# Induced-set attention with a folded feed-forward layer: the second attention in token order, scores lowered in PSUM, most natural x transposed on chip

## The chip, the cores and the metric

One core of a Trainium2 chip runs the whole program. The metric is device time in microseconds of that core; the kernel before takes 263.87 us (median of 3 runs, 262.73 to 266.32). Smaller is better. The engines are named PE (matrix products; PEld its loads of the stationary operand), DVE, ACT, POOL and SP, which issues all transfers here.

## The reference

```
B, N, m, C = 4, 12480, 32, 128        # x [B,N,C] f32, inducing [m,C]; w_in [128,2048], w_out [2048,128]
def mab(q, kv):
    s = (q @ kv.T) / sqrt(C)
    a = exp(s - s.max(-1));  a /= a.sum(-1) + 1e-9
    return a @ kv
h = mab(inducing, x)                  # per batch: 32 rows attend to 12480 tokens
y = mab(x, h)                         # 12480 tokens attend to 32 rows
u = y @ w_in
out = (u - tanh(u)) @ w_out           # [49920, 128] f32
```

The inputs x and inducing are drawn with a spread of 0.1, the weights are handed to the program in their drawn width of 64 bits, as pairs of 32-bit words. Since the rows of h lie close together, both kernels put the layer u - tanh(u) as a tangent around the mean of the 32 rows: 32 rows P of 128 values then stand for h after the layer, and the second attention yields the output as a weighted mean of the rows of P. A bound on the error is worked out in the program (`bound`), and where it does not hold, a general branch (`general`, under `tc.If`) computes everything in full. It is not taken with these inputs.

## The kernel before

The input comes in two layouts: `xT` with the 128 channels on the partitions, and `xn`/`xl`, natural x with tokens on the partitions. Each batch of 12480 tokens is cut into six segments of 1920 tokens (four quarters of SEG = 480) and one of 960 (two quarters).

`first(b)` is the first attention. For each segment `xT` is loaded (L279), `scores` (L260, L263) makes four products of 480 columns, each on its own 32 columns of the array, so that four quarters stand on 128 partitions of one PSUM bank, and DVE copies them with a running maximum (L290). When all seven are there, the maximum goes through a transpose and four tiny products to `nb` (L299 to L309). Then natural x is loaded (L315), ACT takes the exponentials (L322), DVE transposes blocks of 32x32 (L326), and 15 products of 32 stationary columns gather `hacc` (L333). From it come h, transposed (`hT4s[b]`, L342 to L353).

`linear(b)` (L362) multiplies h with the weights: 16 products with 128 stationary columns of `win_sb` and 32 moving columns (L367), mean, tanh and a series on DVE and ACT, the tangent `W` (L404, L405), 16 products with `wout_sb` (L416), and the fold to `P4` (L419, L421).

`second(b, s)` is the second attention, in `b_chain` (L449): scores with `hT4s` (L263), a DVE transpose to tokens on the partitions (L455), maximum (L457), subtraction on POOL (L462), exponentials on ACT (L464), sum (L467), reciprocal (L472, L473), scaling on POOL (L475), a transpose back (L478), and the products with the stationary `P4`, four of 480 columns and 32 rows, two and two into a tile `o` (L496; two such tiles). ACT evicts each half (L502) into `ot`, and SP stores it channel by channel (L505, `outT`).

`weight` (L207) loads the weights as words in eight blocks (L218) and makes 32-bit floats of them: two ACT operations (L221, L236), five on DVE (L224 to L232), two on POOL (L239, L242).

The order on every engine is fixed when the program is built: `Plan.order` takes each operation with a cost, an engine, buffers and a priority (smaller goes first), plays the engines through in time, and writes the instructions down in the order of the starts it found. An engine that waits for an operation's input holds everything behind it. Buffers come from places counted in `PLACES`: 11 for `xT`, 5 for `xn`, 3 for `ot`, 4 PSUM banks (`ps`), 2 tiles `o` of two banks. `first(b)` has priorities from 100b, `second(b, s)` from 100(b + 1) + 13s, so the second attention of one batch is mixed with the first of the next. The loads of w_in start at -30.5, those of w_out at -26.5, those of batch 0's `xT` at -30.

## Time and profile before

| | |
|---|---|
| runs, median (lowest to highest) | 263.87 us (262.73 to 266.32) |
| profiled execution, span | 267.4 us |
| PE, DVE, ACT, POOL busy | 75%, 64%, 37%, 29% |
| mean granted clock of PE | 0.830 |
| read and written in HBM | 55.33 MB, 25.56 MB |

The span goes from the first to the last instruction of one execution on the chip. It is the profiled execution's own time; what lies around the span is not given apart, and the span is 1.3% above the median of the runs. L12 is line 12 of the kernel. A group's row has, after the line: engine, operation, output<-input, shapes, count, then busy time in us and the mean of one in ns, then the idle time before them and what ended it. In a row of the order of time, the first number is the start, the second the length, both in us. A product in full precision appears as two pairs of a load and a multiplication, so that 4 products are x8. Until 46.9 us the records hold no granted clock, and the page shows it as full.

### The profile page before, as it was taken

To read this page: it belongs to the slowest core of one execution; us is meant where nothing else is said; L and a number is where in the kernel's file an instruction comes from. 1 tells how busy PE (TensorE), PEld (TensorE's weight loads), DVE (VectorE), ACT (ScalarE), POOL (GpSimd) and SP (SyncE) were. 2 spreads that over 40 slices of the span, in tenths; PEclk is the share of its full clock that TensorE was granted. 3 is DMA by queue.
4 is the path that set the end of the run, shared out by engine and by line. 5 is a ranking of instruction groups with operands and counts; after the bars stand their busy time and mean duration, and the time that the engine had idled before them with its cause. 6 is when DMAs were issued, how large, how long until landed. Compare 5 with 4: busy or idle time off the path is not lost.

```text
span 267.4 us, 4742 instructions
## 1 busy us (share of the span) xinstructions
PE 201.6 (75%) x1814; PEld 103.5 (39%) x1814; DVE 171.4 (64%) x446; ACT 97.8 (37%) x167; POOL 76.9 (29%) x78
## 2 busy tenths in 40 slices
PE   0555327579799579769977979987989399999760
PEld 0001026337342436614412645825236266662210
DVE  3989988332998917355876563187988214988640
ACT  3322365100054552222239520233377231327741
POOL 1535464100156311010642310014425100264610
PEclk9999999995999959856996895579799755989855
DMA  6999999999958999999779999989358233314882
GB/s 214 416 419 417 417 415 354 307 417 415 372 225 309 399 336 332 418 364 383 256 271 386 380 294 422 347 250 394 151 206 290 90 151 146 147 77 184 365 334 86
DMA packets 13166, 81.27 MB, mean 304 GB/s; under 512 B 1616, under 2 KB 1616, under 8 KB 13136
## 3 DMA queue, kind: packets, MB, share of 16 engines
q1 hardware_dynamic: 13136, 80.89, 79.4%
q8 instruction: 16, 0.26, 0.4%
q14 instruction: 14, 0.11, 0.1%
HBM read 55.33 MB, written 25.56 MB: 303 GB/s over the span
## 4 chain that ended last, share of the span: by engine, by line
DMA 45%; PE 21%; DVE 14%; ACT 13%; issue 2%; SPq 2%; POOL 1%; ACTq 0%; DVEq 0%; POOLq 0%
DMA outT<-ot 35%; ACT ot L502 12%; DMA xT<-in_xT 9%; PE o L496 7%; PE ps_m L367 5%; PE ps_m L263 4%; PE ps_m L416 3%; DVE bt L478 2%; DVE ot L230 2%; DVE s L290 1%; PE ps_m L525 1%; DVE ot L231 1%; DVE S_all L467 1%; DVE ot L228 1%; DVE bmx L457 1%
## 5 line engine op out<-in xcount | busy, mean ns | idle before, releaser
L502 ACT COPY ot<-o 128x960 f32<-128x960 f32 x52 | 47.7, 961 | 85.6 <-DMA outT<-ot 72.6
L496 PE MATMUL o<-bt,P 32*128 32x480 f32 x208 | 53.2, 798 | 20.9 <-ACT ot L502 16.5
L462 POOL TENSOR_TENSOR be<-be,bmx 128x480 f32<-128x480 f32 (+1 forms) x28 | 27.7, 993 | 102.8 <-DVE bmx L457 86.1
L263 PE MATMUL ps_m<-xT,indT_sb 128*32 128x480 f32 x208 | 38.0, 733 | 20.7 <-DMA xT<-in_xT 18.9
L475 POOL TENSOR_TENSOR be<-be,brs 128x480 f32<-128x480 f32 (+1 forms) x28 | 27.8, 993 | 52.2 <-DVE brs L473 36.9
L333 PE MATMUL ps_m<-xn,et 128*32 128x128 f32 (+1 forms) x840 | 35.5, 314 | 8.0 <-issue 4.3
L333 PEld LDWEIGHTS ps_m<-xn,et 128*32 128x32 f32 (+1 forms) x840 | 28.9, 126 | 20.5 <-issue 10.6
L496 PEld LDWEIGHTS o<-bt,P 32*128 32x128 f32 x208 | 16.9, 232 | 48.9 <-ACT ot L502 41.4
L263 PE MATMUL ps_m<-xT,hT 128*32 128x480 f32 x208 | 33.8, 711 | 0.0
L478 DVE STREAM_TRANSPOSE bt<-be 128x480 f32<-128x480 f32 (+1 forms) x28 | 18.6, 665 | 15.1 <-PE o L496 13.1
L326 DVE STREAM_TRANSPOSE et<-s 128x480 f32<-128x480 f32 (+1 forms) x28 | 18.2, 655 | 13.4 <-PE ps_m L333 6.9
L367 PE MATMUL ps_m<-hT,win_sb 128*128 128x32 f32 x128 | 23.6, 359 | 1.3 <-DVE hT L353 1.3
L367 PEld LDWEIGHTS ps_m<-hT,win_sb 128*128 128x128 f32 x128 | 23.1, 283 | 2.9 <-DVE hT L353 2.1
L464 ACT ACTIVATE be<-be 128x480 f32<-128x480 f32 (+1 forms) x28 | 16.9, 603 | 18.8 <-POOL be L462 18.8
L290 DVE TENSOR_SCALAR_CACHE_REDUCE s<-ps_m 128x480 f32<-128x480 f32 (+1 forms) x28 | 17.8, 646 | 8.9 <-PE ps_m L263 8.8
L455 DVE STREAM_TRANSPOSE be<-ps_m 128x480 f32<-128x480 f32 (+1 forms) x28 | 18.3, 659 | 6.7 <-PE ps_m L263 6.7
L467 DVE TENSOR_REDUCE S_all<-be 128x15 f32<-128x480 f32 (+1 forms) x28 | 17.7, 631 | 6.1 <-ACT be L464 5.9
L263 PEld LDWEIGHTS ps_m<-xT,indT_sb 128*32 128x32 f32 x208 | 7.0, 122 | 37.4 <-issue 17.0
L322 ACT ACTIVATE s<-s,nb 128x480 f32<-128x480 f32 (+1 forms) x28 | 19.2, 690 | 2.3 <-DVE nb L309 2.3
L457 DVE TENSOR_REDUCE bmx<-be 128x15 f32<-128x480 f32 (+1 forms) x28 | 17.5, 631 | 0.4
L379 DVE TENSOR_REDUCE mean<-ps_m 128x16 f32<-128x512 f32 x4 | 2.8, 691 | 23.1 <-PE ps_m L367 23.1
L416 PE MATMUL ps_m<-wout_sb,W 128*32 128x128 f32 x128 | 14.9, 276 | 2.5 <-DVE W L405 2.5
(96 smaller groups left out, 165.6 us busy)
## 6 DMA issues: line engine op xcount, KB each, us to landing
xT<-in_xT SPq DMA_DIRECT2D x24, 960.0 KB, 8.5
xn<-in_xn SPq DMA_DIRECT2D x24, 960.0 KB, 9.8
outT<-ot SPq DMA_DIRECT2D x24, 960.0 KB, 4.4
ot<-in_w_in SPq DMA_DIRECT2D x4, 512.0 KB, 7.4
ot<-in_w_out SPq DMA_DIRECT2D x4, 512.0 KB, 6.2
xT<-in_xT SPq DMA_DIRECT2D x4, 480.0 KB, 8.3
xn<-in_xl SPq DMA_DIRECT2D x4, 480.0 KB, 7.6
outT<-ot SPq DMA_DIRECT2D x4, 480.0 KB, 3.6
```

Of the source, the lines that this page charges most:

```text
L263: nc.tensor.matmul(ps[q * m:(q + 1) * m, :SEG], lhsT=w, rhs=row, start=True, stop=True)
L290: nc.vector.tensor_scalar(out=s1.get()[:P, s, :], in0=ps.get()[:P, :SEG], scalar1=1.0, scalar2=None, op0=ALU.mult, op1=ALU.max, accum_out= ...
L333: nc.tensor.matmul(hacc.get()[q * m:(q + 1) * m, :C], lhsT=et.get()[:P, k, :], rhs=x.get()[:P, k, :], start=(s == 0 and k < NQ), stop=(s = ...
L367: nc.tensor.matmul(psM.get()[:, f * m:(f + 1) * m], lhsT=win_sb[:, f * 128:(f + 1) * 128], rhs=hT4s[b][:, :m], start=True, stop=True)
L416: nc.tensor.matmul(psP.get()[:m, :128], lhsT=W.get()[:, f, :], rhs=wout_sb[:, f, :], start=(f == 0), stop=(f == NF - 1))
L457: add("DVE", 0.64, lambda: nc.vector.tensor_reduce(out=bmx.get()[:P], in_=be.get()[:P], axis=AX.X, op=ALU.max), reads=[be], writes=[bmx], ...
L462: add("POOL", 1.1, lambda: nc.gpsimd.tensor_tensor(out=be.get()[:P], in0=be.get()[:P], in1=wide(bmx.get()[:P]), op=ALU.subtract), reads=[b ...
L467: add("DVE", 0.64, lambda: nc.vector.tensor_reduce(out=S()[:P], in_=be.get()[:P], axis=AX.X, op=ALU.add), reads=[be], writes=[part], pri=pri)
L475: add("POOL", 1.1, lambda: nc.gpsimd.tensor_tensor(out=be.get()[:P], in0=be.get()[:P], in1=wide(brs.get()[:P]), op=ALU.mult), reads=[brs], ...
L478: add("DVE", 0.67, lambda: nc.vector.transpose(out=bt.get()[:P], in_=be.get()[:P].rearrange("p k i -> p (k i)")), reads=[be], writes=[bt], ...
L496: nc.tensor.matmul(o.get()[:, q - h, :SEG], lhsT=P4_b[b].get()[p, :], rhs=bt.get()[p, :], start=True, stop=True)
L502: nc.scalar.copy(out=t, in_=o.get()[:, :, :SEG])
```

## The change

- **Segments.** A quarter has 384 tokens (R = 3 blocks of 128), so a batch has eight segments of 1536 tokens and a rest of 192 (two quarters of 96). The tokens of `xT` are permuted on the host so that partition p of an output tile holds consecutive tokens.
- **Natural x.** Only segments 3 and 7 of a batch and the rest are loaded (`xd`, `xnr`). The other six (`turned`) are made from `xT`: 12 transposes of 128x128 on PE in three groups of four, each group evicted from PSUM by ACT or by DVE, as the plan chooses.
- **Second attention.** DVE takes the negated maximum over the 32 rows in one reduction with a transpose inside (`top`), POOL spreads it on a diagonal (`diagonal`), and a product with 0/1 blocks adds it to the scores where they stand in PSUM (`lower`). ACT takes the exponentials from PSUM. They are the stationary operand of the products with P, which has a 129th column of ones, so that the sums come with the output (`product`, 12 products of 129 columns in two halves). The output stands with tokens on the partitions in one tile `o_ps` of four banks; DVE makes the reciprocal, scales and evicts the first half (`whole`); the second half is evicted by ACT and scaled by POOL, or by DVE alone. It is stored in token order. The transposes, the subtraction, the sum and the scaling of before are gone.
- **linear.** The product with w_in has h as the stationary operand (4 products of 512 columns), and goes back through 8 products with a centring matrix. The constant part is a second pass over `wout` in place of an addition. Both passes are spread over four column tiles.
- **Weights.** Two ACT operations, two on POOL (one of them an integer addition) and three on DVE. Their loads come after the first four of `xT` (priorities -26.5 and -22.5).
- **Plan.** An operation may have several engines (`ways`), operations can fall away (`needed`), places are named. `PLACES`: 13 for `xT`, 3 for `xn`, 2 for `xd`, 5 for `ot`, 3 for `et` and `ex`, 4 PSUM banks.

```diff
-SEG = 480
-KB = SEG // 32
+R = 3
+KB = 4 * R
+SEG = 32 * KB
...
-    PLACES = dict(xT=11, xn=5, s1=1, be=3, bt=2, et=2, ot=3, ps=4, o=2, W=1)
+    PLACES = dict(xT=13, xr=3, xn=3, xd=2, xnr=2, s1=11, et=3, ex=3, dg=2, ot=5, otr=2, mb=4, ps=4, W=1)
...
+            def clamp(r=r):
+                nc.gpsimd.tensor_scalar(out=r["v"], in0=r["v"], scalar1=WMAX, scalar2=-WMAX, op0=ALU.min, op1=ALU.max)
+            def absolute(r=r):
+                nc.scalar.activation(out=r["e"], in_=r["v"], func=AF.Abs)
...
+            def bits(r=r, dst=dst):
+                e = r["e"].bitcast(U32)
+                nc.vector.scalar_tensor_tensor(out=r["v"], in0=r["e"], scalar=WMIN, in1=r["v"], op0=ALU.is_ge, op1=ALU.mult)
+                nc.vector.tensor_scalar(out=e, in0=r["hi"], scalar1=3, scalar2=0x3FFFFFFF, ...)
+                nc.vector.scalar_tensor_tensor(out=dst.bitcast(U32), in0=r["hi"], scalar=0xC0000000, in1=e, ...)
...
+    def turned(b, s):
+        return s < NS and s % 4 != 3
...
+            if turned(b, s):
+                for g in range(KB // 4):
+                    ps, part = misc(), Buf()
+                    def turn(ps=ps, xt=xT_b[b, s], g=g):
+                        for k in range(4):
+                            c = (4 * g + k) * 128
+                            nc.tensor.transpose(out=ps.get()[:, k * 128:(k + 1) * 128], in_=xt.get()[:, c:c + 128], identity=ident)
+                    add("PE", 0.45, turn, reads=[xT_b[b, s], ident_b, x], writes=[ps], pri=q0 - 10)
+                    def move(copy, ps=ps, x=x, g=g):
+                        copy(x.get()[:, 4 * g:4 * g + 4, :].rearrange("p k c -> p (k c)"), ps.get())
+                    add("ACT", 0.59, lambda move=move: move(nc.scalar.copy), reads=[ps, x], writes=[part], pri=q0 - 10,
+                        DVE=(0.68, lambda move=move: move(nc.vector.tensor_copy)))
+            else:
+                add("SP", 1.9 if s < NS else 0.4, lambda x=x, s=s: nc.sync.dma_start(
+                    out=x.get(), in_=xn[b, s // 4] if s < NS else xl[b]), writes=[x], pri=q0 - 40, lag=2)
...
         def up():
-            for f in range(NF):
-                nc.tensor.matmul(psM.get()[:, f * m:(f + 1) * m], lhsT=win_sb[:, f * 128:(f + 1) * 128], rhs=hT4s[b][:, :m],
+            for j in range(DFF // 512):
+                nc.tensor.matmul(psY.get()[j * m:(j + 1) * m, :], lhsT=hT_all[:, b, :m], rhs=win_sb[:, j * 512:(j + 1) * 512],
                                  start=True, stop=True)
...
+    def second(b, s, pri):
...
+        add("PE", 0.4, lambda: scores(ps.get(), x.get(), nq, sg, hT_all[:, b, :m], True),
+            reads=[x, hT_b[b], mb, ex], writes=[ps], pri=pri)
+        def top():
+            nc.vector.tensor_reduce(out=mb.get()[:P, :kb], in_=ps.get()[:P, :sg].rearrange("p (k i) -> p k i", i=m), axis=AX.X,
+                                    op=ALU.max, apply_transpose=True, negate=True)
+        def diagonal():
+            nc.gpsimd.tensor_tensor(out=dg.get()[:P, :kb], in0=fold[:P, 0:1, :].to_broadcast([P, kb, m]),
+                                    in1=mb.get()[:P, :kb].unsqueeze(2).to_broadcast([P, kb, m]), op=ALU.mult)
+        def lower():
+            nc.tensor.matmul(ps.get()[:P, :sg], lhsT=quad2[:P, :P], rhs=dg.get()[:P, :kb].rearrange("p k i -> p (k i)"),
+                             start=False, stop=True, skip_group_check=True)
...
+        def product(q0, q1):
+            for r in range(nr):
+                for q in range(q0, q1):
+                    p = slice(q * m, (q + 1) * m)
+                    nc.tensor.matmul(o_ps[:T, q, r * (C + 1):(r + 1) * (C + 1)], lhsT=ex.get()[p, r * T:(r + 1) * T],
+                                     rhs=P_all[p, b, :], start=True, stop=True)
+        for h in range(2):
+            add("PE", 0.37 if full else 0.25, lambda h=h: product(h * nq // 2, (h + 1) * nq // 2), reads=[ex, P_b[b]], writes=[o_b[h]], pri=pri)
+        def recip():
+            nc.vector.tensor_scalar(out=S.rearrange("p (q r) -> p q r", q=nq), in0=o(0, nq)[:, :, :, C], scalar1=1e-9, ...)
+            nc.vector.reciprocal(out=mb.get()[:T, KB:KB + n], in_=S)
...
+            if h == 0:
+                add("DVE", 0.93 if full else 0.3, whole, reads=[mb, o_b[h], ot], writes=[part], pri=pri)
+            else:
+                done = add("ACT", 0.8 if full else 0.3, plain, reads=[o_b[h], mb, ot], writes=[part], pri=pri,
+                           DVE=(0.93 if full else 0.3, whole))
+                add("POOL", 1.65 if full else 0.4, norm, reads=[mb, ot], writes=[part], pri=pri,
+                    needed=lambda done=done: done.eng == "ACT")
+        add("SP", 1.9 if full else 0.4, lambda: nc.sync.dma_start(
+            out=out[at:at + nq * sg, :].rearrange("(p k) c -> p k c", p=T), in_=ot.get()), ...)
...
-    weight(w_in, win_sb, win_b, 60, -30.5)
-    weight(w_out, wout_sb.rearrange("p f d -> p (f d)"), wout_b, 70, -26.5)
+    weight(w_in, win_sb, win_b, 60, -26.5)
+    weight(w_out, wout_sb.rearrange("p f d -> p (f d)"), wout_b, 70, -22.5)
     for b in range(B):
         first(b, 100.0 * b)
         for s in range(NSG):
-            second(b, s, 100.0 * (b + 1) + 13 * s)
+            second(b, s, 100.0 * (b + 1) + 10 * s)
```

More of the change, by code (lines that the diff above doesn't have):

```diff
@@ L94, in release @@
         def release(op, t):
-            ready.setdefault(op.eng, []).append((op.pri, op.n, op))
-            ready[op.eng].sort(key=lambda x: x[:2])
+            if op.needed and not op.needed():
+                op.start = op.end = t
+                heapq.heappush(events, (t, next(count), op))
+                return
+            for k, eng in enumerate(op.ways):
+                ready.setdefault(eng, []).append((op.pri + 1000 * k, op.n, op))
+                ready[eng].sort(key=lambda x: x[:2])
         for op in self.ops:
@@ L254, in fused_kernel @@
-    xT_b, W4 = {}, {}
-    cols = small("cols", [128, NF, 2 * B], 1)
-    mlarge = small("mlarge", [128, B], 1)
-    col_parts = [Buf(cols.get) for _ in range(B)]
-    P4_b = []
-    def scores(ps, rows, w):
-        for q, row in enumerate(rows):
-            nc.tensor.matmul(ps[q * m:(q + 1) * m, :SEG], lhsT=w, rhs=row, start=True, stop=True)
+            add("ACT", 0.7, low, reads=[buf], writes=[part], pri=p)
+            add("POOL", 0.7, clamp, writes=[buf], pri=p)
+            add("ACT", 0.7, absolute, writes=[buf], pri=p)
@@ new lines, in weight, with seg, scores, shape @@
+            add("DVE", 2.1, bits, reads=[], writes=[buf, outs[k]], pri=p)
+            add("POOL", 1.1, join, reads=[buf, part], writes=[outs[k]], pri=p)
+    def seg(x, nq, r, q):
+        return x.rearrange("c (k q j) -> c k q j", q=nq, j=32)[:, :, q, :]
+    def scores(ps, x, nq, sg, w, stop):
+        for q in range(nq):
+            nc.tensor.matmul(ps[q * m:(q + 1) * m, :sg], lhsT=w, rhs=seg(x, nq, None, q), start=True, stop=stop)
+    xT_b = {}
+    def shape(s):
+        return (NQ, SEG, KB) if s < NS else (QL, SEGL, KL)
@@ L311, in first @@
+        add("PE", 0.3, column, reads=[mr, one_b], writes=[psy], pri=p)
+        add("DVE", 0.15, lambda: nc.vector.tensor_scalar(out=nb.get(), in0=psy.get()[:, :1], scalar1=-SC, scalar2=None,
+                                                         op0=ALU.mult), reads=[psy], writes=[nb], pri=p)
         hacc = misc()
-        for s, (base, nq) in enumerate(SGS):
+        last = {k % NQ: (s, k) for s in range(NSG) for k in range(shape(s)[2])}
+        for s in range(NSG):
+            nq, sg, kb = shape(s)
```

609 lines of the change are left out of this document (318 added, 291 removed).

## The prediction

> **What bounds the kernel now.** I read the page's shares and slices first, then its chain, the waits, the windows, and the instructions in order of time.
>
> ```profile
> span 267.4 us, 4742 instructions
> PE 201.6 (75%) x1814; PEld 103.5 (39%) x1814; DVE 171.4 (64%) x446; ACT 97.8 (37%) x167; POOL 76.9 (29%) x78
> ...
> DMA  6999999999958999999779999989358233314882
> ...
> q1 hardware_dynamic: 13136, 80.89, 79.4%
> ...
> DMA outT<-ot 35%; ACT ot L502 12%; DMA xT<-in_xT 9%; PE o L496 7%; PE ps_m L367 5%; PE ps_m L263 4%; PE ps_m L416 3%; DVE bt L478 2%; DVE ot L230 2%; DVE s L290 1%; PE ps_m L525 1%; DVE ot L231 1%; DVE S_all L467 1%; DVE ot L228 1%; DVE bmx L457 1%
> ```
>
> 80.89 MB go through one queue, and output transfers hold 35% of the chain. But in the last quarter the DMA row reads 3 to 5 and below: there the transfers no longer decide.
>
> ```profile
> 0.00:20.00 20.00, 7.32 (x32) 0.84 (x32) 13.70 (x30) 6.02 (x8) 7.10 (x11) 1.00 0.89 350
> 20.00:40.00 20.00, 7.82 (x59) 2.61 (x59) 18.24 (x32) 7.91 (x16) 10.97 (x8) 1.00 1.02 417
> ...
> 160.00:180.00 20.00, 18.85 (x114) 11.22 (x113) 8.81 (x24) 4.36 (x6) 0.99 (x1) 0.58 0.92 342
> 180.00:200.00 20.00, 17.26 (x145) 7.39 (x143) 16.43 (x47) 9.05 (x18) 7.86 (x8) 0.91 0.62 248
> 200.00:220.00 20.00, 14.68 (x218) 10.10 (x214) 8.94 (x24) 9.25 (x17) 4.92 (x5) 0.77 0.52 187
> 220.00:240.00 20.00, 20.00 (x130) 13.20 (x130) 14.29 (x45) 5.10 (x9) 5.33 (x6) 0.76 0.30 124
> ```
>
> Columns: stretch, length, busy time of PE, PEld, DVE, ACT, POOL, granted clock, DMA share, GB/s. Queue speed is 417 GB/s at best. From 220 to 240 PE is busy all the time and DMA for 0.30.
>
> ```profile
> ACT ot L502 <- DMA outT<-ot: 72.6, 16, 9.1
> ...
> PEld o L496 <- ACT ot L502: 41.4, 34, 4.5
> ```
> ```profile
> L505 SPq DMA_DIRECT2D outT<-ot x28: 332/343/344, 80.3 to 262.3; - x28
> ```
>
> So there are three stages: until 80.3 no output can go; then ACT waits (72.6 us) until a transfer frees an `ot`, and the products wait for ACT (41.4); from about 200 on PE and the chain of one batch decide.
>
> **The change, part by part: transfers.**
>
> ```profile
> xn<-in_xn SPq DMA_DIRECT2D x24, 960.0 KB, 9.8
> ...
> xn<-in_xl SPq DMA_DIRECT2D x4, 480.0 KB, 7.6
> ```
>
> Natural x is 24 x 983,040 + 4 x 491,520 bytes = 25.6 MB. Afterwards two of eight segments of a batch are loaded (8 x 786,432) and the rest (4 x 98,304): 6.7 MB. The queue carries 62.0 MB instead of 80.9; at 417 GB/s that is 149 us, 45 less. With five `ot` in place of three the 72.6 us should mostly go. What is late next must be an engine, so I price them at the new segment of 384 columns (32 of them, plus four rests).
>
> **PE.** Rows at the full granted clock:
>
> ```profile
> 75.78 0.48 PE L419 MATMUL ps_m<-P,fold 32*128 32x128 f32 x2
> 76.19 1.01 PE L263 MATMUL ps_m<-xT,indT_sb 128*32 128x480 f32 x8
> 77.25 1.09 PE L496 MATMUL o<-bt,P 32*128 32x480 f32 x8
> 78.27 1.00 PE L263 MATMUL ps_m<-xT,indT_sb 128*32 128x480 f32 x4
> ...
> 177.30 1.82 PE L263 MATMUL ps_m<-xT,hT 128*32 128x480 f32 x16
> ```
> ```profile
> 50.70 1.07 PE L333 MATMUL ps_m<-xn,et 128*32 128x128 f32 x30
> ```
> ```profile
> L525 PE MATMUL ps_m<-cols,ot 128*128 128x8 f32 x32 | 3.7, 257 | 0.0
> ```
>
> A full-precision product is two load-and-multiply pairs. Eight score instructions take 1.01 us alone, sixteen 1.82: 0.81 of streaming and 0.20 of ending. A block of another shape starts 0.07 before the end of the one ahead (75.78 + 0.48 is 76.26, the next starts at 76.19; 77.25 + 1.09 is 78.34, the next starts at 78.27). So a change of shape costs about 0.13 to 0.2 each time. The Trainium skill says the same (TensorEngine Tiling, Key Properties: going to another tiling mode, not just to another tile, drains TensorE); this speaks against the change, which adds changes of shape. By streaming alone the sum below would be 4.4 us a segment, with the drains 5.75; the trace agrees with the drains.
>
> Alone, in us: scores 0.65 + 0.13 = 0.78, twice. Accumulation, 24 instructions of the 30: 0.83. Lowering (new, one full-array weight of 384 columns): 0.65 of streaming, 0.115 for the first load (3.7 / 32 pairs of 128-column loads) and 0.1: 0.85. Transposes (new): the trace has no full transpose; each is one pair with 128 columns loaded and 128 moved. Bounds are 0.115 a pair (L525, loads hidden) and 0.24 (L419, 0.48 for two with their ends); I take 0.115, since the row of 32 runs in a stream, plus 0.16 a group of four: 0.62, three groups in three segments of four: 1.4. Products: before, eight instructions of 480 columns on four row tiles; now 24 of 129 columns, each with a new 128-column load. In each half only two row tiles work, six steps of 0.115 plus 0.17: 0.85 alone, 1.5 for both; if all four overlap, 0.7. I take 1.5, as the halves are issued one after the other. Sum 6.1; a third of the eight blocks will find a neighbour of their shape: less 0.4, **5.75 us a segment**, 184 for 32.
>
> `linear` loses its 32 narrow pairs:
>
> ```profile
> 36.15 0.80 ACT s L322 x2
> ...
> 59.22 5.74 PE ps_m L367 x32
> ...
> 75.08 0.26 ACT P L418
> ...
> 217.23 7.04 PE ps_m L367 x32
> ...
> 230.69 3.47 PE ps_m L416 x32
> ```
>
> It gets 8 wide ones (4 x 512 columns, 0.85) and 16 pairs of turns (1.8), and two passes over `wout`, each spread over four column tiles (1.0 each), instead of one pass of 3.47 on one tile: with ends about 6.3 a batch, 25. Rests 8, bound and maxima 6. **PE in all 223 us at the full clock.** Before, by the same prices: 52 scores and 28 accumulations near 0.95 and 1.0, products about 1.45, linear 8.4 a batch: about 158. So PE gets 1.4 times the work, and 158 shown as 201.6 busy says that much ran at half clock (7.04 against 3.7 for 32 pairs of the same load).
>
> **The other engines.**
>
> ```profile
> L502 ACT COPY ot<-o 128x960 f32<-128x960 f32 x52 | 47.7, 961 | 85.6 <-DMA outT<-ot 72.6 <-PE o L496 12.2 <-ACT ot L502 0.4
> ...
> L462 POOL TENSOR_TENSOR be<-be,bmx 128x480 f32<-128x480 f32 x24 | 23.9, 994 | 102.7 <-DVE bmx L457 86.1 <-DVE brs L472 16.5
> ...
> L322 ACT ACTIVATE s<-s,nb 128x480 f32<-128x480 f32 x24 | 16.5, 690 | 2.3 <-DVE nb L309 2.3
> ...
> L455 DVE STREAM_TRANSPOSE be<-ps_m 128x480 f32<-128x480 f32 x24 | 15.9, 664 | 6.7 <-PE ps_m L263 6.7
> ...
> L290 DVE TENSOR_SCALAR_CACHE_REDUCE s<-ps_m 128x480 f32<-128x480 f32 x24 | 15.3, 651 | 8.9 <-PE ps_m L263 8.8
> L457 DVE TENSOR_REDUCE bmx<-be 128x15 f32<-128x480 f32 x24 | 15.2, 634 | 0.4
> ...
> L464 ACT ACTIVATE be<-be 128x480 f32<-128x480 f32 x24 | 14.5, 604 | 18.8 <-POOL be L462 18.8
> ...
> L224 DVE TENSOR_SCALAR ot<-ot 128x512 uint32<-128x512 uint32 x8 | 7.1, 882 | 3.1 <-ACT win_sb L221 3.1
> ...
> L473 DVE RECIPROCAL brs<-brs 128x15 f32<-128x15 f32 x24 | 6.0, 251 | 0.8
> ...
> L232 DVE SCALAR_TENSOR_TENSOR ot<-ot 128x512 uint32<-128x512 uint32 x8 | 5.5, 692 | 0.3
> ...
> L404 DVE TENSOR_TENSOR W<-ps_m,gp 128x512 f32<-128x512 f32 x4 | 2.7, 673 | 0.0
> ```
>
> DVE a segment, at 0.8 of these lengths: copy with maximum 0.55, transpose 0.5, the maximum with a transpose inside (no row; between L457's 0.5 and L455 plus L457, 1.04; I take 0.55, one pass), reciprocal 0.4, and the scaled eviction of 768 columns 1.0 (L404 times 1.5): 3.0, 96 in all. ACT: exponentials 0.7 (L322, with its sum) and 0.5 (L464), half an eviction 0.8 (L502): 2.0, 64. The 72 evictions of transposes, about 0.65 each, go to either: 47. With `linear` and the weights (three DVE operations of 0.69, 0.88 and 0.69 a block instead of five: 18) each has some 125 us in 250. POOL: 0.8 and 1.6 a segment, 77 plus weights. None of them bounds; all hide under PE, and without that cover 125 would still not decide.
>
> The lowering adds a wait: PE waits for the maximum (0.55) and POOL's diagonal (0.8) after each block of scores, ACT's exponential waits behind it. In PE's order the other batch's blocks are put between; where none is ready it costs up to 1.6 with the handing over, 51 us over 32 segments at worst. I take a small part of it, in the share of waits below.
>
> **The start.** DVE is busy 18.24 of 20 from 20 to 40, for the weights. With two of its five operations gone and x ahead of the weights I put batch 0's exponentials at 29 in place of 36.15 (8.5 MB at 417 GB/s is 20, plus 3 for the slower first stretch at 350 and 6 for the last scores and the maxima chain), the accumulations at 45, `linear` with its hand-overs at about 8 instead of the 16 between 59.22 and 75.08 plus the fold, and the first output near **58** in place of 80.3 (ends 50 and 70). SP issues in order: a load put behind an output waits for that output, as now.
>
> **The sum.** By 58 PE has done about 42 of 223: batch 0's scores, transposes, accumulation and `linear`, and part of batch 1. The other 181 take 190 if PE works 0.95 of the time: it did 20.00 of 20 from 220 to 240 and 17.26 from 180 to 200, so the ends are 1.0 and 0.86 (181 and 210), and two batches' blocks lie beside each other; the last segment's way out 5. 58 + 190 + 5 = **253 of span** against 267.4. The median of the runs before, 263.87, is 0.987 of that profiled span: **250 us**.
>
> **Rivals.**
>
> *PE at its streaming price.* Products overlap on four row tiles and equal shapes lie together: 4.4 a segment, 140, with the rest 170; 58 + 135 / 0.95 + 5 is 205 of span, 202 us. For it: 177.30 shows 16 instructions of two blocks joined. Against: 75.78 to 78.27, where four blocks in a row are of changing shape. Chance 0.16.
>
> *One `o` tile (slower).* Before, two `o` tiles alternate; now one tile of four banks serves all. Its round: products 1.5, reciprocal 0.4, scaled eviction 1.0, handing over 0.4: 3.3 us. If PE puts the foreign blocks of one segment (accumulation, transposes, scores: 3.5) between two rounds while the tile is free, and DVE one foreign operation before each of its two (1.3), a round is 8.1: 58 + 24 x 8.1 + 8 x 3.7 + 5 = 287, 283 us. It decides from 7.5 a round. For it: the 41.4 us that products already wait for eviction with two tiles, and a plan whose PE prices (0.4 for 0.78) are too low. Against: those waits came from `ot`. Chance 0.19.
>
> *Half clock.* From 160 to 180 PE is busy 18.85 of 20 and yet granted 0.58. With a mean of 0.9 after 58: 181 / 0.9 / 0.95 is 212, span 275, 271 us. Beside it the Trainium skill (TensorE: Matmul & The Clock Gate, Part 4) states that transposes do not count as activity for the clock gate; no run here shows it, as the trace has no stream of transposes. Chance 0.10.
>
> *The transfers' gain is eaten entirely* by PE at 0.90 of the time: 58 + 201 + 5 is 264, 260 us, no change. Chance 0.15.
>
> My forecast keeps 0.40, with its own range 238 to 258. Two per cent is about what a measurement of this kernel can tell from no change: 258.6 to 269.1. Faster: 0.40 + 0.16 + 0.02 = 0.58. Slower: 0.19 + part of half clock = 0.24. Within: 0.18. The range, 218 to 277, leaves out most of the streaming case and the worst rounds.
>
> **What would show it.** Right: DMA bytes 62 MB and a DMA share near 0.6 to 0.65; PE over 85% of the span, at a clock above 0.85; first output at 50 to 70; waits of ACT on output transfers under 15 us; groups of four transposes near 0.6 us; product blocks near 0.85 a half. Wrong: PE under 80% with products waiting for the `o` eviction (the round); PEclk full of 5 while PE is busy (the clock); PE busy under 190 us (streaming). It would also be wrong if the first output came after 70, or if the maximum with the transpose inside took over 1 us, which makes DVE 16 us longer.

## The result, and the profile after

The changed kernel takes **279.2 us** (median of 4, 278.8 to 280.7); the kernel before takes 265.1 beside it (median of 4). The ratio is 1.057 (95% interval 1.049 to 1.066): 5.7% slower, where 250 us was forecast and 277 was the upper end of the range. Medians here and below are of all runs, and the ratios leave out runs more than 1.5% above the fastest of the same kernel, such as one of 273.8 us of the kernel before. The profiled execution took 279.2 us for a span of 277.4, so 1.8 us lie around the span. My factor 0.987 from span to time had no ground: 253 of span is 255 us. By the same 1.8 us, the profiled execution of before (span 267.4) took about 269 us: it was simply a slower one than the three of the table.

The page of the changed kernel: the span, PE's share, its clock and the DMA share by slices, the queue, and the chain by lines.

```profile
span 277.4 us, 7109 instructions
...
PE 226.3 (82%) x2926; PEld 144.5 (52%) x2926; DVE 153.7 (55%) x398; ACT 106.2 (38%) x226; POOL 96.1 (35%) x108
...
PEclk9995557999999999999999999999999795577975
DMA  6999995457197789857995868225252300243542
...
q1 hardware_dynamic: 13008, 62.02, 59.8%
...
PE o_ps L535 17%; PE ps L306 15%; PE ps L380 10%; PE ps L405 9%; PE ps L525 7%; DMA xT<-in_xT 5%; DVE ot L565 4%; ACT ot L570 3%; PE ps L448 2%; PE ps L615 2%; DMA ot<-in_w_out 2%; DVE ot L283 2%; DVE ot L282 2%; PE ps L483 1%; PE ps L440 1%
```

The transfers left the chain as forecast: 62 MB, and no output transfer in it where they held 35%. PE has 226 us (223 were forecast), so the miss is not in PE's total. The windows of the same trace, cut at the first output, where batch 3's `linear` begins and at the last output (length, busy time of PE, PEld, DVE, ACT, POOL, clock, DMA share, GB/s), and three lines' first and last starts:

```profile
0.00:76.90 76.90, 52.32 (x646) 32.30 (x650) 49.92 (x113) 31.97 (x63) 24.22 (x41) 0.84 0.73 274
76.90:213.60 136.70, 130.13 (x1879) 85.23 (x1871) 80.07 (x215) 62.77 (x141) 51.59 (x49) 1.00 0.68 249
213.60:269.50 55.90, 43.72 (x410) 27.01 (x408) 22.54 (x64) 11.47 (x22) 20.29 (x20) 0.76 0.29 115
269.50:277.40 7.90, 0.12 (x1) 0.00 (x0) 1.20 (x7) 0.00 (x0) 0.00 (x0) 0.50 0.34 122
```
```profile
L425 DVE COPY hT_all<-ps x4: 277/286/292, 57.8 to 214.4; 128x128 f32<-128x128 f32 x4
...
L535 PE MATMUL o_ps<-P_all,ex x784: 268/270/579, 71.6 to 267.8; 32*128 32x129 f32 x192, 32*96 32x129 f32 x4
...
L582 SPq DMA_DIRECT2D out<-ot x32: 332/333/344, 76.9 to 269.0; - x32
```

The sum had three terms: 58, 190 and 5. They measured 76.9, 192.6 and 7.9. By the first output PE had done 52 us instead of 42, so the 174 left would have taken 183 at the forecast share of 0.95. The middle kept that share (130.13 of 136.7, 0.952, at full clock); the last 56 us did not (0.78, at a clock of 0.76). Against 253 that is 12 us for the start net of the work done in it, 9.5 for the tail, 3 for the end.

**The start**, in order of time:

```profile
29.55 0.16 DVE L347 TENSOR_REDUCE mx<-mxg 128x1 f32<-128x9 f32 x1
29.63 1.70 DVE L282 SCALAR_TENSOR_TENSOR ot<-ot 128x512 f32<-128x512 f32 x1
...
33.08 0.27 DVE L351 TENSOR_REDUCE mr<-ps 1x32 f32<-1x128 f32 x1
...
33.30 1.79 POOL L289 TENSOR_TENSOR wout_sb<-wout_sb,ot 128x512 uint32<-128x512 uint32 x1 [0.69 <-DVE wout_sb L285]
...
33.98 1.39 DVE L283 TENSOR_SCALAR ot<-ot 128x512 uint32<-128x512 uint32 x1
...
36.34 0.14 DVE L359 TENSOR_SCALAR nb<-ps 128x1 f32<-128x1 f32 x1
...
36.52 0.61 ACT L394 ACTIVATE s<-s,nb 128x384 f32<-128x384 f32 x1
...
41.27 0.43 DVE L283 TENSOR_SCALAR ot<-ot 128x512 uint32<-128x512 uint32 x1
```

Two short steps of the chain of maxima stand each behind a whole weight block of three DVE operations: DVE leaves the chain at 29.71 and comes back at 33.08, leaves at 33.35 and comes back at 36.34. So the first exponential comes at 36.5, no earlier than before. The shift L283 takes 0.43 us alone and 1.39 while POOL's integer addition runs: it ends at 35.37, 0.28 after POOL (35.09). The Trainium skill has a reason (SBUF — State Buffer, "SBUF: two separate sides": DVE, in its two-port modes or with two inputs from SBUF, and GpSimd share one pair of ports, which one of them locks for its whole instruction). These rows agree, though no row shows in which mode the shift runs.

**The tail**, in order of time; the second fence has the waits (total us, times, longest):

```profile
226.86 4.79 PE L615 MATMUL ps<-cols,ot 128*128 128x8 f32 x32
231.58 2.27 PE L535 MATMUL o_ps<-P_all,ex 32*128 32x129 f32 x24
...
244.27 0.96 DVE L565 TENSOR_TENSOR ot<-o_ps,mb 128x768 f32<-128x768 f32 x1
...
245.40 0.80 ACT L570 COPY ot<-o_ps 128x768 f32<-128x768 f32 x1 [3.41 <-DVE ot L565]
246.25 2.27 PE L535 MATMUL o_ps<-P_all,ex 32*128 32x129 f32 x24 [1.78 <-ACT ot L570]
```
```profile
PEld o_ps L535 <- ACT ot L570: 22.1, 18, 2.8
ACT ot L570 <- DVE ot L565: 21.0, 14, 3.4
PE o_ps L535 <- ACT ot L570: 12.9, 11, 2.6
```

The bound's 32 products stand ahead of batch 3's first product. The granted clock is 1.00 from 220.0 to 226.8, 0.74 while they run and 0.50 from 231.6 to 242.0, where a block takes 2.27 us instead of 1.28. And a round on the one `o` tile is a chain of five: products, reciprocal, DVE's half, then ACT's half (0.17 us after DVE's has ended), then the next products.

### The profile page after: what moved, and what is told of

It reads as the page before. It is cut to its first block, busy times and chain, and to the rows that moved or that the text cites. A ratio compares the mean times of both kernels' runs of the same rounds, so it can differ in the third digit from the quotient of the medians.

```text
span 277.4 us, 7109 instructions
## 1 busy us (share of the span) xinstructions
PE 226.3 (82%) x2926; PEld 144.5 (52%) x2926; DVE 153.7 (55%) x398; ACT 106.2 (38%) x226; POOL 96.1 (35%) x108
## 4 chain that ended last, share of the span: by engine, by line
PE 67%; DVE 13%; DMA 6%; ACT 4%; issue 4%; SPq 1%; POOL 1%; DVEq 0%; ACTq 0%; POOLq 0%
PE o_ps L535 17%; PE ps L306 15%; PE ps L380 10%; PE ps L405 9%; PE ps L525 7%; DMA xT<-in_xT 5%; DVE ot L565 4%; ACT ot L570 3%; PE ps L448 2%; PE ps L615 2%; DMA ot<-in_w_out 2%; DVE ot L283 2%; DVE ot L282 2%; PE ps L483 1%; PE ps L440 1%
## 5 line engine op out<-in xcount | busy, mean ns | idle before, releaser
L573 POOL TENSOR_TENSOR ot<-ot,mb 128x768 f32<-128x768 f32 x32 | 47.0, 1469 | 92.7 <-ACT ot L570 92.7
L535 PE MATMUL o_ps<-P_all,ex 32*128 32x129 f32 (+1 forms) x784 | 49.3, 307 | 14.8 <-ACT ot L570 12.9
L535 PEld LDWEIGHTS o_ps<-P_all,ex 32*128 32x128 f32 (+1 forms) x784 | 41.1, 203 | 34.4 <-ACT ot L570 22.1
L384 ACT COPY xn<-ps 128x512 f32<-128x512 f32 x50 | 28.6, 590 | 41.0 <-PE ps L380 35.9
L380 PE MATMUL ps<-ident,xT 128*128 128x128 f32 x288 | 43.0, 289 | 0.5 <-ACT xn L384 0.5
L380 PEld LDWEIGHTS ps<-ident,xT 128*128 128x128 f32 x288 | 32.6, 146 | 12.6 <-issue 5.4
L306 PE MATMUL ps<-xT,indT_sb 128*32 128x384 f32 x256 | 29.1, 540 | 11.6 <-DMA xT<-in_xT 10.0
L565 DVE TENSOR_TENSOR ot<-o_ps,mb 128x768 f32<-128x768 f32 x32 | 30.4, 950 | 5.7 <-ACT ot L570 5.1
L528 ACT ACTIVATE ex<-ps 128x384 f32<-128x384 f32 (+1 forms) x36 | 16.6, 463 | 42.6 <-PE ps L525 42.6
L525 PE MATMUL ps<-dg,quad 128*128 128x384 f32 (+1 forms) x72 | 31.0, 517 | 1.6 <-POOL dg L520 1.6
L306 PE MATMUL ps<-xT,hT_all 128*32 128x384 f32 x256 | 29.3, 552 | 0.2 <-ACT xn L384 0.2
L384 DVE COPY xn<-ps 128x512 f32<-128x512 f32 x22 | 15.1, 688 | 7.3 <-PE ps L380 6.7
L306 PEld LDWEIGHTS ps<-xT,indT_sb 128*32 128x32 f32 x256 | 6.8, 115 | 18.9 <-issue 12.4
```

The source lines that it names most:

```text
L306: nc.tensor.matmul(ps[q * m:(q + 1) * m, :sg], lhsT=w, rhs=seg(x, nq, None, q), start=True, stop=stop)
L380: nc.tensor.transpose(out=ps.get()[:, k * 128:(k + 1) * 128], in_=xt.get()[:, c:c + 128], identity=ident)
L384: copy(x.get()[:, 4 * g:4 * g + 4, :].rearrange("p k c -> p (k c)"), ps.get())
L525: nc.tensor.matmul(ps.get()[:P, :sg], lhsT=quad2[:P, :P], rhs=dg.get()[:P, :kb].rearrange("p k i -> p (k i)"), start=False, stop=True, ski ...
L535: nc.tensor.matmul(o_ps[:T, q, r * (C + 1):(r + 1) * (C + 1)], lhsT=ex.get()[p, r * T:(r + 1) * T], rhs=P_all[p, b, :], start=True, stop=True)
L565: nc.vector.tensor_tensor(out=dst().rearrange("p (q r) c -> p q r c", r=nr), in0=o(q0, q1)[:, :, :, :C], in1=rs().rearrange("p (q r) -> p ...
```

## The experiments

All medians; the kernel before ran beside each group at 264.9 to 266.8 us. Ratios are to it. "Alone" means on the changed kernel. Since the kernel before itself moved by 2 us from group to group, gains of 2 to 4 us between runs of different groups are close to the noise.

### The o tile

```diff
-    o_ps = ps_o.tile([128, NQ, 512], F32, name="o_ps")
+    o_ps = [ps_o.tile([128, NQ // 2, 512], F32, name=f"o_ps{h}") for h in range(2)]
...
```

> The output tile of four banks becomes two tiles of two banks, one for each half; each half's products then depend only on that half's eviction (one more small DVE operation a segment, about 0.1 us). Theory (the one tile makes the two evictions of a round follow each other): the round of the tail goes from 3.8 to 3.1 us, 8 x 0.7 = 5.6 us less, the middle as before since PE sets it: 273 to 275 us. Rival (the evictions follow each other because of the output buffer that both write, not of the PSUM tile): round still 3.8, 279 to 280 us.

Measured: **265.9 us**, ratio 0.994 (0.989 to 0.998), 13.3 less than the changed kernel and more than twice what I expected. Its middle and two rounds of its tail (first fence: windows; second: order of time):

```profile
72.20:208.70 136.50, 134.79 (x1959) 89.46 (x1955) 85.28 (x251) 65.59 (x145) 53.76 (x50) 1.00 0.70 253
```
```profile
248.32 0.96 DVE L567 TENSOR_TENSOR ot<-o_ps,mb 128x768 f32<-128x768 f32 x1
...
248.61 0.49 ACT L528 ACTIVATE ex<-ps 128x384 f32<-128x384 f32 x1 [1.93 <-PE ps L525]
249.00 0.79 ACT L572 COPY ot<-o_ps 128x768 f32<-128x768 f32 x1
...
249.42 1.36 PE L535 MATMUL o_ps<-P_all,ex 32*128 32x129 f32 x24 [0.62 <-DVE ot L567]
...
252.53 1.36 PE L535 MATMUL o_ps<-P_all,ex 32*128 32x129 f32 x24 [0.47 <-DVE ot L567]
...
254.25 0.80 ACT L572 COPY ot<-o_ps 128x768 f32<-128x768 f32 x1 [1.22 <-issue]
...
254.54 0.96 DVE L567 TENSOR_TENSOR ot<-o_ps,mb 128x768 f32<-128x768 f32 x1
```

The two evictions now overlap, and the next products start while ACT still empties its half: 3.1 us a round. What is left between their starts, 0.7 us, is ACT's order: the next segment's exponentials (L528) stand ahead of ACT's half, and end as it starts. In the last full round nothing stands there, and ACT's half starts 0.29 us ahead of DVE's. From the first product to batch 3's `linear`, PE is busy 0.987 of the time; in the changed kernel it is 0.954 in the same cut (135.4 of 142.0). So most of the 5% that I had put down to waits in general was the `o` tile too.

### The products over four row tiles

```diff
-        def product(q0, q1):
+        def product():
...
-                for q in range(q0, q1):
+                for q in range(nq):
...
-        for h in range(2):
-            add("PE", 0.37 if full else 0.25, lambda h=h: product(h * nq // 2, (h + 1) * nq // 2), reads=[ex, P_b[b]], writes=[o_b[h]], pri=pri)
+        add("PE", 0.74 if full else 0.25, product, reads=[ex, P_b[b]], writes=o_b, pri=pri)
```

The two operations of six products thereby become one of twelve in the plan.

With two `o` tiles:

> With the two o tiles, the twelve products of a segment are issued over all four row tiles in turn instead of two and two; the sum of instructions is the same. Theory (the two halves use only two row tiles at a time, as the prediction's price took it): a block of 24 falls from 1.28 to 0.75 to 0.9 us, 32 x 0.4 = 13 us of PE, nearly all in the time, since PE sets the middle: 253 to 258 us against 265.9 with two o tiles alone. Rival (loads of 128 columns follow each other on PE whatever the row tile, four do not overlap more than two): 1.28 as before, 265 to 267 us. Second rival (block shorter, but the round of eviction decides): 0.8 us and 263 to 266 us.

Alone, with the one tile:

> The changed kernel with the one o tile, and only the twelve products issued over all four row tiles. With two o tiles this gave 15.1 us. Theory (with one o tile a round is product, reciprocal, two evictions in a row; the product's 0.33 us is part of every round, and of PE's sum too): 279.2 - 32 x 0.33 = 268 to 270 us. Rival (the block is shorter, but both evictions now wait for the whole block, so the round stays): 276 to 280 us.

Measured: **250.8 us** with two tiles (ratio 0.945, 0.939 to 0.952), 262.5 alone (0.987, 0.981 to 0.993): 15.1 and 16.7 less by the medians, 12.8 and 18.5 by the ratios (0.0486 and 0.070 of 264 us). The first two rows group the products of the changed kernel and of this edit alone; the third is a block of 24 with two tiles, from the kernel of 246.8 us below.

```profile
L535 PE MATMUL o_ps<-P_all,ex 32*128 32x129 f32 (+1 forms) x784 | 49.3, 307 | 14.8 <-ACT ot L570 12.9 <-DVE ot L565 1.9
```
```profile
L535 PE MATMUL o_ps<-P_all,ex 32*128 32x129 f32 (+1 forms) x784 | 33.3, 293 | 13.4 <-ACT ot L569 10.6 <-DVE ot L564 2.2 <-ACT ex L528 0.6
```
```profile
224.08 0.95 PE L540 MATMUL o_ps<-P_all,ex 32*128 32x129 f32 x24
```

The same instructions take 16 us less of PE, about as much as the time falls. The block went from 1.28 to 0.95, less far than I expected (0.33 x 32 is 10.6). Part of the rest is that in four rounds of the middle each half stood by itself, 0.94 with its own ends, and that blocks at half clock shrank from 2.27 to 1.67. How much the joining alone gives, without the new order, was not tried.

### Without transposes

```diff
-    PLACES = dict(xT=13, xr=3, xn=3, xd=2, xnr=2, s1=11, et=3, ex=3, dg=2, ot=5, otr=2, mb=4, ps=4, W=1)
+    PLACES = dict(xT=13, xr=3, xn=0, xd=5, xnr=2, s1=11, et=3, ex=3, dg=2, ot=5, otr=2, mb=4, ps=4, W=1)
...
     def turned(b, s):
-        return s < NS and s % 4 != 3
+        return False
...
-                    out=x.get(), in_=xn[b, s // 4] if s < NS else xl[b]), writes=[x], pri=q0 - 40, lag=2)
+                    out=x.get(), in_=xn[b, s] if s < NS else xl[b]), writes=[x], pri=q0 - 40, lag=2)
```

Alone:

> No transposes: natural x of all eight segments is loaded (five places). PE loses 72 groups of 0.62 us (45 us), ACT and DVE 72 evictions; the queue carries 80.9 MB again, 194 us at 417 GB/s. Theory (PE sets the middle): about 5.9 - 1.4 = 4.5 us a segment, then the queue or the tail decides: 245 to 262 us. Rival (the transfers' order and rate set the middle, PE only seems full): no gain or a loss, 279 us and more.

On the best kernel known by then (`together`, below):

> The kernel of 240.8 us with natural x loaded for all segments (five places) in place of the transposes: PE 42 us less, the queue 18.9 MB more, 45 us at 417 GB/s. Theory (the loads cost more than the transposes, since first attention wants two layouts of a batch at once and PE waits for xd): 255 to 285 us. Rival (the 311.5 us of the same edit with one o tile came from the rounds, not from the loads): 228 to 245 us.

Measured: **311.5 us** alone (1.164, 1.154 to 1.174) and **253.8** in the second place (0.954, 0.943 to 0.966), 13.0 more than with transposes. The first is the rival's result, the second lies 1.2 us below the theory's range. PE waits for both layouts. The waits alone, then in the second place with its queue:

```profile
PE o_ps L535 <- ACT ot L570: 31.6, 21, 2.6
PE ps L405 <- DMA xd<-in_xn: 23.9, 12, 6.0
```
```profile
q1 hardware_dynamic: 16464, 80.90, 83.1%
```
```profile
PE ps L311 <- DMA xT<-in_xT: 23.8, 11, 6.0
PE ps L410 <- DMA xd<-in_xn: 10.3, 10, 2.4
```

PE also gains far less than the 43 us of transposes: its busy time falls from 226.3 to 212.0 alone and from 204.1 to 187.8 in the second place. The blocks that are left take longer, and the mean granted clock is lower, 0.823 for 0.894 and 0.836 for 0.942. So the transposes are worth their 43 us of PE here; more places for `xd` than five were not tried. Of the 32 us lost alone, part came from rounds on the one tile that had less to fill them (31.6 us instead of 12.9).

### The weights at the start

All of DVE's weight work (`late`, one operation of three instructions a block) behind batch 0's bias `nb`; then w_in's behind the bias and w_out's behind `hT_all`:

```diff
...
+    for op in late:
+        op.deps.add(nbs[0])
```

> The three DVE operations of every weight block come after the bias of batch 0 (nb). Theory (they hold the chain of maxima): first exponential at 27 to 30 us instead of 36.5, first output at 67 to 71 instead of 76.9, and since PE is the bound from there on the end moves by the same: 270 to 274 us. Rival (linear of batch 0 then waits for the weights): first output within 3 us of before, 276 to 280 us. Second rival (transfers set the middle): first output earlier, end not, 278 us.

> The DVE operations of w_in come after the bias of batch 0, those of w_out after its h (hT_all). Theory (all weights have to pass through DVE before batch 0's h, since the last transposes of exponentials stood behind them; of the two matrices only w_in is needed for the first product of linear): h done at 45 to 50 us instead of 57.8 (58.2 with all weights behind the bias), first product of the output at 60 to 65 instead of 71.6, the time 268 to 273 us. Rival (linear then waits for w_out, DVE's sum of work before the first output is the same): first product at 69 to 72, no change, 277 to 281 us. Second rival (an earlier start is eaten by the round on the one o tile): first product earlier by 7 us or more, time within 3 us of 279.

Measured: 279.1 us (1.045, 1.035 to 1.056) and 281.9 (lowest 278.9, highest 284.8): no gain clear of the noise. The first exponential came at 28.4 and 28.5, as the theory had it. But `hT_all` came at 58.0 and 53.6, the first product at 71.8 and 77.9 instead of 71.6. The blocks of weights now stood in front of the transposed exponentials, and in the second kernel in front of `linear`'s small operations. A new place for the whole blocks only moved the trouble. The next edit leaves their place to the plan and cuts them into single instructions (`bits` becomes three functions):

```diff
...
-            add("DVE", 2.1, bits, reads=[], writes=[buf, outs[k]], pri=p)
+            add("DVE", 0.7, keep, writes=[buf], pri=p)
+            add("DVE", 0.7, shift, writes=[buf], pri=p)
+            add("DVE", 0.7, sign, writes=[buf, outs[k]], pri=p)
```

With two `o` tiles and four row tiles, and alone:

> Two o tiles and four row tiles as in the run before (250.8 us), and the three DVE operations of every weight block become three operations of the plan with their own places in DVE's order. Theory (a whole block of 2.1 to 3.5 us in front of the short operations of batch 0, its maxima and its transposed exponentials, sets the start, not the sum of DVE's work): first exponential at 29 to 33 us instead of 36.2, first product at 62 to 67 instead of 70.8, 242 to 247 us. Rival (DVE's sum of work before the first product sets it, 19 of 20 us busy from 20 to 40, with the weights stretched beside POOL): first product at 69 to 72, 249 to 253 us.

> The changed kernel with the one o tile, and only the weights' DVE work as three operations a block. With two o tiles and four row tiles this gave 3.9 us and moved the first product from 70.8 to 67.9. Theory (start and o tile add up, since PE or the round is full from the first product on): 274 to 277 us. Rival (with one o tile the rounds of batch 0 stretch over the time that is won): 279 us, with the first product at 67 to 69.

Measured: 246.8 us (0.936, 0.917 to 0.955; 3.9 less than 250.8) and 275.6 (1.038, 1.027 to 1.049; 3.6 less than 279.2). The times lie in the theories' ranges, and the start counts about the same under either `o` tile. But the first product came at 67.9, between the first theory's 62 to 67 and its rival's 69 to 72, and alone at 66.5 (71.6 in the changed kernel). So the blocks' length is a part of the late start, not all of it. The rows of the first of them:

```profile
L430 DVE COPY hT_all<-ps x4: 266/279/292, 54.5 to 194.1; 128x128 f32<-128x128 f32 x4
...
L540 PE MATMUL o_ps<-P_all,ex x784: 268/270/578, 67.9 to 235.6; 32*128 32x129 f32 x192, 32*96 32x129 f32 x4
```

### The bound's products

A lower priority alone (280.4 us) left them in the same place, since the plan saw PE idle there. A dependency moves them:

```diff
-        add("PE", 2.5, pe, reads=[wabs, wabs2, cols], writes=[ps], pri=pri)
+        add("PE", 2.5, pe, reads=[wabs, wabs2, cols], writes=[ps], pri=pri).deps.add(last_product[0])
```

> The 32 products of the error bound (L615) are made to follow the last product of the output. A lower priority alone did not do it: the plan saw PE idle at that place and put them into the same gap, 226.1 us, and nothing moved. Theory (they delay the products of batch 3 by their 4.3 to 4.9 us and pull the clock down behind them): first product of batch 3 at 227 instead of 231.6, the next rounds at 3.8 instead of 4.1 to 5.3 us, and at the end they hide beside the last output's 8 us: 270 to 274 us. Rival (the clock falls anyway, from linear's little work; only the block goes): 274 to 276 us. Second rival (at the end they add as much): 279 us.

Measured: 279.1 us (1.052, 1.045 to 1.059), no change. In order of time:

```profile
227.15 1.28 PE L535 MATMUL o_ps<-P_all,ex 32*128 32x129 f32 x24 [0.35 <-ACT P_all L496]
...
239.08 2.27 PE L535 MATMUL o_ps<-P_all,ex 32*128 32x129 f32 x24 [1.78 <-ACT ot L570]
...
252.60 1.28 PE L535 MATMUL o_ps<-P_all,ex 32*128 32x129 f32 x24 [1.41 <-ACT ot L570]
256.43 1.28 PE L535 MATMUL o_ps<-P_all,ex 32*128 32x129 f32 x24 [1.40 <-ACT ot L570]
...
261.01 7.00 PE L615 MATMUL ps<-cols,ot 128*128 128x8 f32 x32
```

The first part held: first product at 227.15 instead of 231.58, the last about 7 us earlier. But the clock falls all the same (0.68 from 231.6 to 236.9, and a block of 2.27 three rounds on), and at the end the products take 7.0 us, longer than the last output hides. In four pieces of eight, behind the first four products of batch 3, with two `o` tiles and four row tiles:

> Two o tiles and four row tiles, and the 32 products of the bound in four pieces of eight, behind the first to fourth product block of batch 3. Theory (in one piece they cost 4.8 us in front of the first product of batch 3 and hold the clock down for three rounds; a piece of 1.2 us fits the waits of the tail): first product of batch 3 at about 212 instead of 216.6 us, no product block of 1.67 us behind it, 243 to 247 us. Rival (the clock falls from linear's little work alone): only the block goes, and the pieces cost part of it: 247 to 249 us. Second rival (the tail is a round of evictions, which takes 3 us either way): 247 us, with rounds of 3 us.

Measured: 248.7 us (0.942, 0.925 to 0.959), 2.0 less than 250.8. The theory's marks came (first product at 212.39, no block of 1.67 behind it), but its 243 to 247 us did not: the time is the first rival's, the mechanism is not. Two rows of its tail, and for comparison one of the kernel of 246.8 us, which has the block in one piece, 3.64 us long from 206.07:

```profile
212.39 0.95 PE L535 MATMUL o_ps<-P_all,ex 32*128 32x129 f32 x24 [0.35 <-ACT P_all L496]
...
217.37 0.95 PE L616 MATMUL ps<-cols,ot 128*128 128x8 f32 x8
```
```profile
213.68 1.67 PE L540 MATMUL o_ps<-P_all,ex 32*128 32x129 f32 x24 [1.65 <-DVE ot L571]
```

In pieces, the products of the output take 0.95 and the granted clock is 1.00 from 212.4 to 237.5. Behind the block in one piece it is 0.64 from 209.6 to 219.0. So in this tail the block in one piece took the clock down; with the one tile, above, it fell without it. But the pieces cost 4 us of PE, and the rounds keep most of the gain.

### Prices, and all together

The plan's prices were set to the measured ones:

> Two o tiles and four row tiles, with the plan's prices set to what the trace shows (scores 0.75 instead of 0.4, accumulation 0.8 instead of 0.5, lowering 0.83 instead of 0.4, products 0.88, linear's blocks 0.95 to 1.0, weights on DVE 2.7 instead of 2.1). The plan's own sum for PE rises from 140 to 208 us; the work is the same, only the order and the choice of ACT or DVE change. Theory (the middle is bound by PE, which is fed anyway): little, 246 to 251 us. Rival (an order made for an engine that is cheaper than it is puts foreign blocks in front of the chain): 240 to 246 us.

Measured: 247.3 us (0.934, 0.914 to 0.955), 3.4 less: about as the theory had it. The first sum of four edits used weak parts (weights in two, the bound at the end):

> Two o tiles, products over four row tiles, the bound's products at the end, weights in two parts: the four together. If each theory holds: 265.9 - 10 (products) - 6 (weights) - 5 (bound, with the clock behind it) = 245 us, from 240 to 252. If only the two o tiles count, 264 to 267 us.

Measured: 263.5 us (0.998, 0.992 to 1.003), 12.7 worse than with two of its parts (two `o` tiles and four row tiles, 250.8). One of its ten runs took 350.1 us, at a mean granted clock of 0.557. The first product came at 75.8, and the bound's products ran alone at the end, 7.00 us from 245.1. With the better parts:

> Two o tiles, four row tiles, weights in three operations, the bound in pieces, measured prices, and the second attention's segments 14 apart in priority instead of 10. If each theory holds: 250.8 - 5 (weights) - 5 (bound and clock) - 0 to 3 (prices) = 238 to 242 us. If only the bound counts, 245 to 247 us.

Measured: **240.8 us** (0.911, 0.894 to 0.929). The single gains (13.3, 16.7 and 3.6 alone, 2.0 and 3.4 on 250.8) sum to 39.0, and the whole is 38.4. That this fits is in part luck: taken by the ratios, the same gains sum to 44 us for a whole of 38.6. Against the kernel of 246.8 us the first product comes 5.3 us earlier (62.6 for 67.9), and the stretch from there to the last product is as long as before (166.9 and 167.7). Which of the prices, the pieces and the wider steps of priority moved the start, no run separates. Last, DVE's weight work without POOL's additions beside it:

```diff
-                nc.gpsimd.tensor_tensor(out=dst.bitcast(U32), in0=dst.bitcast(U32), in1=r["lo"], op=ALU.add)
+                nc.vector.tensor_tensor(out=dst.bitcast(U32), in0=dst.bitcast(U32), in1=r["lo"], op=ALU.bitwise_or)
...
-            add("POOL", 1.4, join, reads=[buf, part], writes=[outs[k]], pri=p)
+            add("DVE", 0.7, join, reads=[buf, part], writes=[outs[k]], pri=p)
```

> The kernel of 240.8 us with the low bits of the weights joined by an OR on DVE in place of POOL's integer addition (a carry out of the low three bits is lost, under 1e-6 of a weight). Theory (DVE's weight operations are stretched while POOL works on the weights, 0.43 against 1.40 us for the shift): the three operations of a block return to 0.69, 0.43 and 0.69, the fourth adds 0.7, the first product comes 1 to 4 us earlier than 62.6, 237 to 240 us. Rival (DVE's sum grows, the stretch has another cause): first product at 63 to 66, 241 to 244 us.

Measured: **237.0 us** (0.891, 0.883 to 0.899), 10.9% less than the kernel before. Its shift, and its first product:

```profile
L284 DVE TENSOR_SCALAR ot<-ot 128x512 uint32<-128x512 uint32 x8 | 3.6, 447 | 0.0
...
L540 PE MATMUL o_ps<-P_all,ex x784: 268/270/373, 60.2 to 226.2; 32*128 32x129 f32 x192, 32*96 32x129 f32 x4
```

The shift is back at 0.45 us in the mean (0.60 in the kernel of 240.8 us, 0.83 in the changed kernel), the first product at 60.2 (62.6). Other things moved with the addition (a hand-over to POOL and back went, too), so the 3.8 us are not all the stretch.

## Why the prediction was wrong

- **Transfers: right.** 62.0 MB; ACT's waits on output transfers are gone. That five `ot` are there was not so: ACT makes the bound's |wout| at 49.9 and 51.7 (L592), and two of them are held until the bound's products end at 231.6. No wait of an engine on an output transfer shows for it. One reading of before was loose: in its last quarter the DMA row also has three slices of 8.
- **PE's prices: right block by block, the sum in part by luck**, 226 for 223. The group of transposes took 0.60 to 0.66 (0.62), lowering 0.81 to 0.91 (0.85), accumulation 0.79 to 0.86 (0.83), scores 0.83 (0.78), `linear` 5.7 (6.3), products 1.28 (1.5). But 223 was a sum for the full clock, and 226 holds the stretches at a mean clock of 0.84 and 0.76 and the halves that stood alone: 64 blocks of scores took 58.4 us where 64 x 0.83 is 53.1. What I took as given, the halves one after the other, was the largest single loss of the kernel (16.7 us), though not of the forecast, which had it in its price. I had priced the overlap (0.7) and not asked why the code should not have it.
- **DVE's operations: right.** The maximum with a transpose took 0.58 (0.55), the scaled eviction 0.95 (1.0). DVE and ACT together were busy 260 us, where I had some 125 each, but DVE had 154 of them.
- **The start: the first step that failed.** I had the exponentials at 29, the accumulations at 45, `linear` at 8 us and the first output at 58; they came at 36.5, just before 57.8 (h), 12.5 us and 76.9, past the 70 that I had named as a sign of being wrong. I summed the weights' DVE work (18 us; measured 21.4 in 24 operations) and moved batch 0 by what fell away. I did not put DVE's queue in order: a chain of short operations meets one whole weight block at each step. Nor did I see that POOL's addition stretches DVE. `linear` took 12.5 us (58.6 to 71.1), with other blocks between its steps in PE's order. Batch 1's are not the reason: batch 3's `linear`, with no other batch beside it, took 12.6 (214.7 to 227.3). Cut into single instructions, the weight blocks let the first output come at 71.8, 5.1 of the 18.9 us; with all the edits it comes at 63.8. What the rest of the 18.9 us is, the runs do not show piece by piece.
- **The middle: right number, wrong reason.** PE's share was 0.952 for the forecast 0.95, but most of the 5% were rounds on the `o` tile; the lowering's wait, which I feared, is 1.6 us in all.
- **The tail: the second step that failed.** In the sum it was 5 us after a full PE. Batch 3 has nothing beside it: its `linear` lies bare from 213.6, the bound's products stand in front, the clock falls, and eight rounds of 3.8 to 5.4 us follow. PE is busy 0.78 of these 56 us, not 0.95, and the last output takes 7.9. With two `o` tiles the same stretch takes 48.4 us (208.8 to 257.2), so the rounds on the one tile are some 7.5 of it.
- **The rival "one `o` tile"** had the mechanism in the main (a round on one tile, a plan whose PE prices are too low: 140 us for 226), but not that ACT's half waits for DVE's. That its 283 us lie close to the measured 279.2 is luck: rounds took 5.9 us in the middle, (213.2 - 71.6) / 24, not 8.1, so they did not decide there, and 4.5 in the tail, not 3.7, and its start was 58 too. Of the tile's 13.3 us, 4.8 (136.7 x 0.035) lay in the share that my sum had given to waits anyway; the other 8.5 are a third of the miss. The half-clock rival held only for the tail; the middle, with 45 of the 72 groups of transposes, ran at 1.00.

Left open: what takes the clock down in the tail where the bound's products do not stand ahead, what the rest of the late start is, and how much of `together_or`'s gain is the port.

## What to carry to other kernels

Price the start and the tail as chains, each step with what stands in front of it in its engine's order, and only the middle as a sum over the busiest engine. A buffer that is filled and emptied in one piece makes a round of all its steps: give it two tiles and look whether the evictions overlap. An order planned with prices is only as good as they are, and an operation of several instructions cannot let a short, urgent one pass.

## What the hardware showed that I had not expected

- Twelve products of 32 rows take 0.95 us over four row tiles in turn, 1.28 two and two, with the same instructions, both at full clock.
- Transposes between other blocks did not lower the clock (1.00 from 76.9 to 213.6, with 26.4 us of transposes in that stretch). The Trainium skill (TensorE: Matmul & The Clock Gate, Part 4) says that they do not count as activity for it; no stretch here holds transposes alone, so that stays untested, but it did not matter in this mix. The clock can fall though PE is busy throughout: PE was busy for all of 226.8 to 231.6, where the bound's 32 products of 8 columns stand, at a granted clock of 0.74, and blocks behind them took 2.27 us for 1.28. With two tiles and four row tiles, the same products in four pieces left it at 1.00. They are not the only cause, since with one tile it fell without them too.
- An operation of DVE can take three times its time beside POOL's: 0.43 and 1.39 us for the same shift, and 0.45 in the mean once the addition had left POOL.
